# Fused attention and two gated layers: transpositions spread over the short key tiles, in a PSUM bank of their own

## The chip, the cores and the metric

One core of one Trainium2 chip runs the whole program. The metric is the device time of one execution in microseconds (us): the time from the first to the last instruction of that core. The kernel before was timed three times.

## The reference, cut to what matters

```python
q_rot, k_rot = rotate(q), rotate(k)              # (4, 8, 576, 64): 32 heads, 576 tokens, width 64
scores = (q_rot @ k_rot.transpose(0, 1, 3, 2)) / sqrt(64)
scores = scores - max(scores, axis=-1)           # one maximum per query
attn = exp(scores); attn = attn / (attn.sum(-1) + 1e-9)
x = (attn @ v)  -> (2304, 512)
x = (sigmoid(x @ w_gate) * (x @ w_val)) @ w_out  # 512 -> 1536 -> 512
out = elu(x @ w_in) @ w_out2                     # 512 -> 2048 -> 512
```

## The kernel before, in words

All of it is float32. The products must be more exact than one pass of the fast format (F32R), so an operand is split into a high part, rounded to F32R, and a low part, the difference.

**Heads, pairs, slots and steps.** The 32 heads are worked in 16 pairs. One head is one slot of ten steps, and slots follow one another (`scores`, `maxima`, `values`, called from the loop over `n` at the end of the attention part). In step h of slot i TensorE gets, in this order:
- `scores(i, h)` (L434): two products, K1 with Q1 and K2 with Q2, of one key tile and half of the 576 queries. Steps 0 to 3 and 5 to 8 have key tiles of 128 keys, steps 4 and 9 have the short tile of 64 keys. ScalarE takes the exponential. For a short tile it takes two, and VectorE then makes a low part of it (`low_part`, L444, put 1.5 steps later; written p below).
- `maxima(i+2, h)` (L387): one product for the row maxima of the head two slots ahead. Its result is reduced by VectorE (L389). A slot of even number has ten of them, a slot of odd number eight (steps 0 to 7).
- `values` (L463, or L460 and L461 for a short tile): the product with v, five steps behind the scores.

An entry made by `at(slot, step, ...)` runs after that step's products; a step ending in .5 runs ahead of the next step's products. In program order VectorE's queue at the start of a slot thus holds: the reduction of step 0, `join` (L394), p of the last slot's step 9, the reduction of step 1, the evacuation of a `values` result (L477), the copy of the maxima's row (L411, from `max_row`, whose product L409 also takes a tile of `ps_mt`), the reduction of step 2, and one operation of the weights' conversion (L121 to L140). After step 5 come the same conversion, p, a reduction and an evacuation. `max_row` needs `join`, since its stationary operand is what `join` writes.

**Splits.** A pair's rotated q and k have to be transposed and split before its maxima start. `split` does one half of one operand: two transpositions of 128x128 (L331; three where the tails are with it), one ScalarE copy into the high part (L334), one VectorE subtraction into the low part (L335). A pair has four of them and nine transpositions in all. For pair pr the first head is in slot s0 = 2 pr, and all four splits are in slot s0 - 4, an even one, ahead of steps 2, 4, 6 and 8, each followed by its subtraction one step later. Then `move` starts the DMAs that put the parts into W (L347 to L349, on SyncE's queue), and `last_queries` copies a few columns on GpSimd (L401). GpSimd makes the rotated q and k (`rope_ops`, L312 to L316) one to two slots earlier.

**PSUM.** The eight banks are three pools: `ps_mt` three (maxima and `max_row`), `ps_qk` three (scores, and the transpositions of `split`), `ps_pv` two (values). A new tile takes the bank that was released first, and waits for whoever read it last.

After attention, at about 320 us, come the two gated layers, 844 us of products of 128x512.

Of the kernel before, what the change touches and what calls it, by code (L numbers as in the profile page):

```python
# [9 lines left out]
F32 = mybir.dt.float32  # L10
F32R = mybir.dt.float32r
AF = mybir.ActivationFunctionType
ALU = mybir.AluOpType
# [6 lines left out]
def attention_moe_moe_kernel(  # L20
# [15 lines left out]
    nc = tc.nc  # L36
    B, H, S, D = q.shape
    P = 128
# [5 lines left out]
    ST = S // P  # L44
# [140 lines left out]
    banks = ctx.enter_context(ExitStack())  # L185
    with ExitStack() as att:
# [7 lines left out]
        prep = att.enter_context(ExitStack())  # L194
        raw_p = prep.enter_context(tc.tile_pool(name="raw", bufs=2))
        rope_p = prep.enter_context(tc.tile_pool(name="rope", bufs=1))
        ps_mt = banks.enter_context(tc.tile_pool(name="ps_mt", bufs=3, space=bass.MemoryType.PSUM))
        ps_qk = banks.enter_context(tc.tile_pool(name="ps_qk", bufs=3, space=bass.MemoryType.PSUM))
        ps_pv = banks.enter_context(tc.tile_pool(name="ps_pv", bufs=2, space=bass.MemoryType.PSUM))

        raws = {}
# [44 lines left out]
        ident = const.tile([P, P], F32, name="ident")  # L246
# [32 lines left out]
        def operand(i, which, c0, n):  # L279
            c = ("K2", "Q1", "K1", "Q2").index(which) * S + c0  # L280
            return W[i // 2 % NPAR][i % 2][:, c : c + n]
# [5 lines left out]
        def at(slot, step, fn, *args):  # L287
            agenda.setdefault(slot * NSTEP + step, []).append((fn, args))
# [3 lines left out]
        def rope_ops(pr, which, eng):  # L292


            if which == "t":
                x = raw(pr, "kq")
                r = rope_p.tile([P, 2, D], F32, tag="rt", name=f"rt{pr}")
                s = rope_p.tile([P, 2, D], F32, tag="st", name=f"st{pr}")
                rv, sv = r, s
                cos, sin = (tabt[:, j].unsqueeze(1).to_broadcast([P, 2, D]) for j in range(2))  # L300
            else:
                x = raw(pr, which)
                r = rope_p.tile([P, ST, 2, D], F32, tag="r" + which, name=f"r{which}{pr}", bufs=2)
                s = rope_p.tile([P, ST, 2, D], F32, tag="s", name=f"s{which}{pr}")
                rv, sv = (y.rearrange("p t h d -> p h t d") for y in (r, s))
                cos, sin = (tab[:, c].unsqueeze(1).to_broadcast([P, 2, ST, D]) for c in range(2))
            rot[pr, which] = r
            tt = eng.tensor_tensor

            axes = "p n" if which == "t" else "p h t"  # L310
            two = lambda y: y.rearrange(f"{axes} (two d) -> {axes} two d", two=2)
            tt(out=two(sv), in0=two(x)[..., ::-1, :], in1=two(sin), op=ALU.mult)  # L312
            yield
            tt(out=rv, in0=x, in1=cos, op=ALU.mult)
            yield
            tt(out=r, in0=r, in1=s, op=ALU.add)  # L316
            yield

        parts = {}

        def split(pr, which, half, later=None):

            if which == "k" and half == 0:

                parts[pr] = hl_p.tile([P, 4, S], F32R, tag="hl", name=f"hl{pr}")
            tails = which == "k" and half == 1
            c0, n = half * HM, HM + (P if tails else 0)
            T = ps_qk.tile([P, 512], F32, tag="qk", name=f"T{which}{pr}_{c0}")[:, 0:n]
            rows = [rot[pr, which][:, c // P] for c in range(c0, c0 + HM, P)] + ([rot[pr, "t"]] if tails else [])
            for j, r in enumerate(rows):  # L330
                nc.tensor.transpose(T[:, j * P : (j + 1) * P], r.rearrange("p h d -> p (h d)"), ident)  # L331
            c0 += 0 if which == "k" else S + TL
            hi, lo = (parts[pr][:, 2 * j : 2 * j + 2].rearrange("p w s -> p (w s)")[:, c0 : c0 + n] for j in range(2))
            nc.scalar.copy(hi, T)  # L334
            rest = lambda: nc.vector.tensor_tensor(out=lo, in0=T, in1=hi.bitcast(F32), op=ALU.subtract)  # L335
            if later is None:
                rest()
            else:
                at(*later, rest)

        def move(pr, ab):

# [80 lines left out]
        def scores(i, h):  # L423

            a, t = divmod(h, ST + 1)
            n = P if t < ST else TL
            if t == ST:

                p = probs[i, h] = p_p.tile([P, HA], F32R, tag="pt", name=f"p{i}_{h}")[:, 0:HS]
            else:  # L430
                e = probs[i, h] = e_p.tile([P, HA], F32, tag="ef", name=f"e{i}_{h}", bufs=2 * ST)[:, 0:HS]
            s = ps_qk.tile([P, 512], F32, tag="qk", name=f"s{i}_{h}")[0:n, 0:HS]
            for st, mv in (("K1", "Q1"), ("K2", "Q2")):
                nc.tensor.matmul(  # L434
                    s, lhsT=operand(i, st, t * P, n), rhs=operand(i, mv, a * HS, HS), start=st == "K1", stop=st == "K2"
                )
            if t == ST:
                nc.scalar.activation(p[TL:P], s, AF.Exp, scale=SCALE)
                e = s
                at(i, h + 1.5, low_part, e, p)  # L440
            nc.scalar.activation(e, s, AF.Exp, scale=SCALE)  # L441
# [6 lines left out]
        def values(i, h):  # L448


            a, t = divmod(h, ST + 1)
            pr, ab = divmod(i, 2)
            par = pr % 2
            c = slice(a * HS, (a + 1) * HS)
            if t == 0:
                ps[i, a] = ps_pv.tile([P, 512], F32, tag="pv", name=f"pv{i}_{a}")[:, 0:HS]
            out_ps = ps[i, a]
            e = probs.pop((i, h))
            if t == ST:
                nc.tensor.matmul(out_ps[0:D], lhsT=VT[par][:, ab, 0:D], rhs=e, start=False, stop=False)  # L460
                nc.tensor.matmul(out_ps, lhsT=VT[par][:, ab, D : 3 * D], rhs=e, start=False, stop=True)  # L461
            else:
                nc.tensor.matmul(out_ps, lhsT=VF[par][:, ab, t], rhs=e, start=t == 0, stop=False)  # L463
            if t < ST:
                return
            if ab == 0 and a == 0:
                us[pr] = (fin_p if pr == NPAIR - 1 else u_p).tile([P, S], F32, tag="u", name=f"u{pr}")
                sums[pr] = SUM[D * par : D * par + D]
            done = us[pr][D * ab : D * ab + D, c], sums[pr][32 * ab : 32 * ab + 1, c], out_ps
            if (i, a) == (NHEAD - 1, 1):  # L470
                return done
            at(i + 1, 5 * a + 0.5, evacuate, *done, "s")
            at(i + 1, 5 * a + 1, evacuate, *done, "u")
# [63 lines left out]
        at(-5, 4, constants, 1, 1, nc.gpsimd)  # L537
        for which in "kq":
            for half in range(2):
                at(-5, 1, split, 0, which, half)  # L540
            at(-5, 1, copies, 0, which, nc.vector.tensor_copy)
        at(-5, 1, move, 0, 1)
        at(-5, 2, last_queries, 0, nc.scalar.copy)
        at(-2, 19, last_queries, 1, nc.scalar.copy)
        for (which, half), st in zip((("k", 0), ("k", 1), ("q", 0), ("q", 1)), (10, 11, 17, 18)):
            at(-2, st, split, 1, which, half)
        at(-2, 13, copies, 1, "k", nc.scalar.copy)
        at(-2, 19, copies, 1, "q", nc.scalar.copy)
        at(-1, 11, move, 1, 1)
# [1 line left out]
        for pr in range(NPAIR):  # L551
            s0 = 2 * pr
            if pr > 1:
                for j, (which, slot, steps) in enumerate(
                    (
                        ("k", s0 - 6, (8, 8, 9, 9) if pr == 3 else (1,3,6,8)),
                        ("t", s0 - 6, (19,) * 4 if pr == 3 else (9, 9, 9, 9)),
                        ("q", *((0, (0, 0, 3, 3)) if pr == 2 else (s0 - 5, (1,3,6,8)))),
                    )
                ):  # L560
                    gen = rope_ops(pr, which, nc.gpsimd)
                    for st in steps:
                        at(slot, st, pull, gen)
                for j, (which, half) in enumerate((("k", 0), ("k", 1), ("q", 0), ("q", 1))):
                    at(s0 - 4, (6.5, 7.5, 8.5, 9.5)[j] if pr == 2 else (1.5, 3.5, 5.5, 7.5)[j], split, pr, which, half, None if pr == 2 else (s0 - 4, 2.5 + 2 * j))
                at(s0 - 4, 10 if pr == 2 else 9, move, pr, 0)
                at(s0 - 4, 10 if pr == 2 else 9, last_queries, pr, nc.gpsimd.tensor_copy)
                at(s0 - 4, 19, move, pr, 1)
            for piece in range(2 if pr > 0 else 0):
                at(s0 - 1, (5, 7)[piece], split_v, pr, piece)  # L570
        for pr in range(2, NPAIR):
            slot, step = {3: (-1, 9), 4: (1, 3)}.get(pr, (2 * pr - 8, 3))
# [30 lines left out]
        for n in range(-6 * NSTEP, NHEAD * NSTEP + half_slot):  # L603
            i, h = divmod(n, NSTEP)
# [21 lines left out]
        rest = remaining()  # L626
# [179 lines left out]
```

## Time and profile before

| what | value |
|---|---|
| time, median of three executions | 1164.22 us (1162.93 to 1165.01) |
| the profiled execution: span, which is its own time | 1164.2 us |
| TensorE (PE) busy | 1138.5 us, 98% |
| VectorE (DVE) busy | 937.7 us, 81% |
| ScalarE (ACT) / GpSimd (POOL) busy | 451.2 us, 39% / 605.0 us, 52% |
| granted TensorE clock | full in all 40 slices |

The page's busy share of TensorE counts matmuls whose ends are modelled and overlap, so a busy TensorE may still lose time. A better measure here is the distance of one instruction's start from that of the same instruction a slot or a step on. In the timeline view a row is: start in us from the span's start, duration, engine, line, operation, result and operands, shapes, how many were merged into the row, and in brackets the idle time before it and who ended it. In the view by windows a row is: the stretch, its length, then the busy time (and number of instructions) of PE, PEld (weight loads), DVE, ACT and POOL, the granted clock, the DMA engines' busy share and GB/s.

### The profile page before, as it was taken

What the parts mean: (1) busy time and instruction counts of PE and PEld (TensorE: products, weight loads), DVE (VectorE), ACT (ScalarE), POOL (GpSimd) and SP (SyncE); (2) the same over time, 40 slices, a digit from 0 to 9 for tenths busy, and PEclk for the clock granted to TensorE, in tenths of its full rate; (3) what the DMA queues carried; (4) which work ended last, traced back from release to release, by engine and by line L of the source; (5) the groups of instructions that cost most, each with busy time, mean ns of one, the idle gap of its engine ahead of it and who ended that gap; (6) DMA issues with size and microseconds to landing.
All of it is one profiled execution on the core that took longest, in us unless ns stands there. A gap on an engine that the chain in (4) does not pass through costs nothing.

```text
span 1164.2 us, 16786 instructions
## 1 busy us (share of the span) xinstructions
PE 1138.5 (98%) x5728; PEld 960.5 (82%) x5728; DVE 937.7 (81%) x1994; ACT 451.2 (39%) x1037; POOL 605.0 (52%) x695
## 2 busy tenths in 40 slices
PE   5999999999999999999999999999999999999998
PEld 3888888888888888888888888888888888888887
DVE  6768888887876888667777766888999999999844
ACT  4666666667753321221222122344322222222221
POOL 8766666863343554434444435775554545545521
PEclk9999999999999999999999999999999999999999
DMA  6667677767121211111111110111111111110004
GB/s 166 158 161 184 163 179 169 163 158 160 41 94 37 73 55 40 52 37 47 44 38 54 37 55 19 37 37 37 55 37 55 37 37 55 37 55 1 1 37 127
DMA packets 58757, 88.03 MB, mean 76 GB/s; under 512 B 18176, under 2 KB 30736, under 8 KB 58672
## 3 DMA queue, kind: packets, MB, share of 16 engines
q1 hardware_dynamic: 58672, 86.96, 28.2%
q8 instruction: 45, 0.74, 0.3%
q14 instruction: 40, 0.33, 0.1%
HBM read 55.45 MB, written 4.87 MB: 52 GB/s over the span
## 4 chain that ended last, share of the span: by engine, by line
PE 78%; DVE 17%; ACT 2%; issue 1%; DMA 1%; SPq 0%; POOL 0%; POOLq 0%
PE h L647 12%; PE h L648 12%; PE h L649 12%; PE pv L463 9%; PE o L647 7%; PE o L648 7%; PE o L649 7%; PE s L434 7%; DVE z L730 3%; PE mt L387 3%; DVE g L673 2%; DVE g L672 2%; DVE ca L131 2%; DVE cm L140 1%; DVE MX L389 1%; DVE ce L134 1%
## 5 line engine op out<-in xcount | busy, mean ns | idle before, releaser
L679 POOL TENSOR_TENSOR gl<-g,gh 128x512 fp32r<-128x512 f32 (+1 forms) x140 | 168.6, 1204 | 330.2 <-ACT gh L678 261.7
L678 ACT CAST gh<-g 128x512 fp32r<-128x512 f32 (+1 forms) x140 | 81.0, 579 | 308.2 <-DVE g L673 171.1
L434 PE MATMUL s<-W 128*128 128x288 f32 (+1 forms) x640 | 182.0, 366 | 3.8 <-DVE p L444 1.3
L648 PE MATMUL h<-xl,wh 128*128 128x512 f32 (+1 forms) x480 | 176.6, 368 | 0.0
L647 PE MATMUL h<-xh,wh 128*128 128x512 f32 (+1 forms) x480 | 176.6, 368 | 0.0
L649 PE MATMUL h<-xh,wl 128*128 128x512 f32 (+1 forms) x480 | 176.5, 368 | 0.0
L463 PE MATMUL pv<-e,VF 128*128 128x288 f32 x512 | 166.0, 407 | 0.0
L141 POOL TENSOR_TENSOR ca<-ca,wh 128x256 f32<-128x256 f32 x136 | 111.5, 820 | 96.8 <-DVE cm L137 82.4
L389 DVE TENSOR_REDUCE MX<-mt 128x1 f32<-128x288 f32 x288 | 127.5, 450 | 40.9 <-PE mt L387 38.7
L434 PEld LDWEIGHTS s<-W 128*128 128x128 f32 (+1 forms) x640 | 106.1, 182 | 32.1 <-DVE p L444 5.2
L138 ACT CAST wh<-ca 128x256 fp32r<-128x256 f32 x136 | 55.1, 405 | 195.0 <-DVE ca L131 195.0
L143 POOL TENSOR_TENSOR wl<-ca,cm 128x256 fp32r<-128x256 f32 x136 | 111.0, 816 | 18.5 <-DVE cm L140 12.1
L441 ACT ACTIVATE e<-s 128x288 f32<-128x288 f32 x256 | 104.3, 411 | 41.4 <-PE s L434 38.2
L648 PE MATMUL h<-yl,wh 128*128 128x512 f32 (+1 forms) x320 | 117.7, 368 | 0.0
L649 PE MATMUL h<-yh,wl 128*128 128x512 f32 (+1 forms) x320 | 117.7, 368 | 0.0
L647 PE MATMUL h<-yh,wh 128*128 128x512 f32 (+1 forms) x320 | 117.7, 368 | 0.0
L668 DVE TENSOR_TENSOR g<-h,g 128x512 f32<-128x512 f32 (+1 forms) x60 | 38.2, 637 | 95.1 <-PE h L649 92.3
L647 PE MATMUL o<-wh,gh 128*128 128x512 f32 x288 | 112.7, 391 | 1.5 <-DVE z L730 1.2
L648 PE MATMUL o<-wl,gh 128*128 128x512 f32 x288 | 112.2, 389 | 0.0
L649 PE MATMUL o<-wh,gl 128*128 128x512 f32 x288 | 112.1, 389 | 0.0
L649 PEld LDWEIGHTS h<-xh,wl 128*128 128x128 f32 x480 | 90.5, 189 | 15.1
L647 PEld LDWEIGHTS h<-xh,wh 128*128 128x128 f32 x480 | 90.5, 189 | 15.0
(110 smaller groups left out, 2514.4 us busy)
## 6 DMA issues: line engine op xcount, KB each, us to landing
W<-hl SPq DMA_DIRECT2D x90, 288.0 KB
raw<-in_moe_w_out_dram SPq DMA_DIRECT2D x28, 512.0 KB
raw<-in_moe_w_in_dram SPq DMA_DIRECT2D x16, 512.0 KB
raw<-in_moe_w_gate_dram SPq DMA_DIRECT2D x12, 512.0 KB
raw<-in_moe_w_val_dram SPq DMA_DIRECT2D x12, 512.0 KB
rb<-d SPq DMA_DIRECT2D x32, 144.0 KB
k<-in_k_dram SPq DMA_DIRECT2D x16, 256.0 KB
q<-in_q_dram SPq DMA_DIRECT2D x16, 256.0 KB
```

The source lines that it names most:

```text
L138: nc.scalar.copy(h, a)
L141: nc.gpsimd.tensor_tensor(out=a, in0=a, in1=h.bitcast(F32), op=ALU.subtract)
L143: nc.gpsimd.tensor_tensor(out=l, in0=a, in1=mf, op=ALU.add)
L389: nc.vector.tensor_reduce(out=MX[pr % 2][:, a, c : c + 1], in_=m, axis=AX.X, op=ALU.max, negate=True)
L434: nc.tensor.matmul(s, lhsT=operand(i, st, t * P, n), rhs=operand(i, mv, a * HS, HS), start=st == "K1", stop=st == "K2")
L441: nc.scalar.activation(e, s, AF.Exp, scale=SCALE)
L463: nc.tensor.matmul(out_ps, lhsT=VF[par][:, ab, t], rhs=e, start=t == 0, stop=False)
L647: nc.tensor.matmul(ps, lhsT=ah, rhs=bh, start=j == 0, stop=False)
L648: nc.tensor.matmul(ps, lhsT=ah, rhs=bl, start=False, stop=False)
L649: nc.tensor.matmul(ps, lhsT=al, rhs=bh, start=False, stop=j == n - 1)
L678: nc.scalar.copy(hi, g)
L679: nc.gpsimd.tensor_tensor(out=lo, in0=g, in1=hi.bitcast(F32), op=ALU.subtract)
```

## The change

From the fifth pair (pr = 4) on the four splits of a pair are put one to each short key tile of two slots: k's halves to steps 4 and 9 of slot s0 - 5 (odd), q's halves to steps 4 and 9 of slot s0 - 4 (even). Their transpositions are no longer issued together; each is put ahead of one product of the short tile: K1, K2 and the first of `values`. ScalarE's copy follows after the step's products (`finish`), the subtraction 1.5 steps later, but for q's second half at once. Their PSUM tile comes from a new pool `ps_t` of one bank; `ps_mt` has two banks instead of three. `move` of the pair's first head and `last_queries` run one step later. The first two pairs' q second half also takes `ps_t`; pairs 0 to 3 stay where they were.

```diff
-        ps_mt = ...tile_pool(name="ps_mt", bufs=3, space=PSUM)
+        ps_mt = ...tile_pool(name="ps_mt", bufs=2, space=PSUM)
         ps_qk = ...tile_pool(name="ps_qk", bufs=3, space=PSUM)
+        ps_t = ...tile_pool(name="ps_t", bufs=1, space=PSUM)
...
+        between = []
-        def split(pr, which, half, later=None):
+        def split(pr, which, half, pool, tag, later=None, apart=False):
...
-            T = ps_qk.tile([P, 512], F32, tag="qk", ...)[:, 0:n]
+            T = pool.tile([P, 512], F32, tag=tag, ...)[:, 0:n]
...
+            def finish():
+                assert not between
+                nc.scalar.copy(hi, T)
+                if later is None:
+                    rest()
+                else:
+                    at(*later, rest)
+            for j, r in enumerate(rows):
+                if apart:
+                    between.append((turn, (j, r)))
+                else:
+                    turn(j, r)
+            if apart:
+                at(*apart, finish)
+            else:
+                finish()
+        def one_between():
+            if between:
+                fn, args = between.pop(0)
+                fn(*args)
...
             for st, mv in (("K1", "Q1"), ("K2", "Q2")):      # scores
+                if t == ST:
+                    one_between()
                 nc.tensor.matmul(s, ...)
...
             if t == ST:                                      # values
+                one_between()
                 nc.tensor.matmul(out_ps[0:D], ...)
...
-                    at(s0 - 4, (6.5, ...)[j] if pr == 2 else (1.5, 3.5, 5.5, 7.5)[j], split, pr, which, half,
-                       None if pr == 2 else (s0 - 4, 2.5 + 2 * j))
-                at(s0 - 4, 10 if pr == 2 else 9, move, pr, 0)
-                at(s0 - 4, 10 if pr == 2 else 9, last_queries, pr, nc.gpsimd.tensor_copy)
+                    if pr < 4:
+                        ...                                  # as before, from ps_qk
+                    else:
+                        slot, step = s0 - 5 + j // 2, 4 + 5 * (j % 2)
+                        at(slot, step - 0.5, split, pr, which, half, ps_t, "t",
+                           (slot, step + 1.5) if j < 3 else None, (slot, step))
+                at(s0 - 4, 10 if pr == 2 or pr > 3 else 9, move, pr, 0)
+                at(s0 - 4, 10 if pr == 2 or pr > 3 else 9, last_queries, pr, nc.gpsimd.tensor_copy)
```

## Rows read from the trace of the kernel before

**Rows 1.** The page: its first line.

```profile
span 1164.2 us, 16786 instructions
```

**Rows 2.** By windows: the odd slot 17, and slot 28, even and without a split.

```profile
184.79:193.03 8.24, 8.24 (x52) 7.29 (x51) 7.12 (x18) 5.54 (x16) 8.00 (x12) 1.00 0.54 108
...
285.38:293.85 8.47, 8.47 (x53) 7.52 (x52) 6.73 (x18) 5.61 (x15) 0.00 (x0) 1.00 0.63 141
```

**Rows 3.** By windows: the twelve even slots 4 to 26; slots 6 and 24, and the sum.

```profile
80.69:91.72 11.03, 10.36 (x63) 8.29 (x61) 7.99 (x23) 7.05 (x19) 4.12 (x6) 1.00 0.61 141
...
248.54:258.97 10.43, 10.01 (x62) 8.29 (x61) 9.34 (x22) 7.04 (x19) 7.40 (x10) 1.00 0.52 115
...
sum 123.63, PE 118.66 PEld 99.27 DVE 103.89 ACT 85.16 POOL 66.66; mean PE 9.89 PEld 8.27 DVE 8.66 ACT 7.10 POOL 5.55
```

**Rows 4.** Timeline of PE in the even slot 16 (174.16 to 184.79).

```profile
178.01 0.38 PE L331 MATMUL Tk<-ident,rk 128*128 128x128 f32 x2
178.23 0.27 PE L331 MATMUL Tk<-ident,rt 128*128 128x128 f32 x1
...
180.32 0.41 PE L331 MATMUL Tq<-ident,rq 128*128 128x128 f32 x2 [0.29 <-ACT e L441]
...
182.03 0.53 PE L434 MATMUL s<-W 128*128 128x288 f32 x2 [0.42 <-DVE p L444]
```

**Rows 5.** Timeline of DVE in slot 16.

```profile
178.20 0.41 DVE L335 TENSOR_TENSOR hl<-Tk,hl 128x256 fp32r<-128x256 f32 x1
178.53 0.86 DVE L389 TENSOR_REDUCE MX<-mt 128x1 f32<-128x288 f32 x2
179.31 0.55 DVE L335 TENSOR_TENSOR hl<-Tk,hl 128x384 fp32r<-128x384 f32 x1
179.78 0.45 DVE L389 TENSOR_REDUCE MX<-mt 128x1 f32<-128x288 f32 x1
180.14 1.36 DVE L121 TENSOR_SCALAR ce<-raw 128x256 int32<-128x256 int32 x1
181.53 0.45 DVE L444 TENSOR_TENSOR p<-s,p 64x288 fp32r<-64x288 f32 x1
```

**Rows 6.** Timeline of POOL in slot 24: the end of pair 14's rotated q.

```profile
249.59 1.27 POOL L316 TENSOR_TENSOR rq<-rq,sq 128x512 f32<-128x512 f32 x1
```

**Rows 7.** By windows: the last 2 us of slot 17.

```profile
191.00:193.03 2.03, 2.03 (x15) 1.76 (x14) 1.70 (x5) 1.08 (x4) 1.87 (x3) 1.00 0.00 0
```

**Rows 8.** Timeline of ACT where slot 17 begins: a copy, and step 9's second exponential.

```profile
183.44 0.37 ACT L334 CAST hl<-Tq 128x256 fp32r<-128x256 f32 x1 [0.42 <-PE Tq L331]
...
184.90 0.39 ACT L441 ACTIVATE s<-s 64x288 f32<-64x288 f32 x1
```

**Rows 9.** Timeline of DVE at the start of slot 17: reductions of steps 0 and 1.

```profile
185.38 0.46 DVE L389 TENSOR_REDUCE MX<-mt 128x1 f32<-128x288 f32 x1 [0.20 <-PE mt L387]
...
186.32 0.44 DVE L389 TENSOR_REDUCE MX<-mt 128x1 f32<-128x288 f32 x1
```

**Rows 10.** Timeline of PE in slot 17: the maxima's product of step 2.

```profile
186.94 0.29 PE L387 MATMUL mt<-W 128*128 128x288 f32 x1
```

**Rows 11.** Timeline of DVE in slot 28: p, and the conversion after step 5.

```profile
286.53 0.45 DVE L444 TENSOR_TENSOR p<-s,p 64x288 fp32r<-64x288 f32 x1
...
290.63 0.42 DVE L131 SCALAR_TENSOR_TENSOR ca<-ce,cm 128x256 f32<-128x256 int32 x1
```

**Rows 12.** Timeline of PE in slot 28: the maxima's products of steps 2 and 8.

```profile
287.50 0.29 PE L387 MATMUL mt<-W 128*128 128x288 f32 x1
...
292.58 0.29 PE L387 MATMUL mt<-hl,QT 128*128 128x288 f32 x1
```

**Rows 13.** Timeline of DVE in slot 8: the conversion after step 5.

```profile
106.35 0.85 DVE L137 TENSOR_SCALAR cm<-ca 128x256 int32<-128x256 int32 x1
```

**Rows 14.** Timeline of DVE at the start: the first head's reductions.

```profile
14.56 3.94 DVE L389 TENSOR_REDUCE MX<-mt 128x1 f32<-128x288 f32 x10 [0.76 <-PE mt L387]
```

**Rows 15.** Timeline of DVE where slot 8 begins (99.95).

```profile
101.19 0.21 DVE L495 RECIPROCAL r<-r 128x9 f32<-128x9 f32 x1 [1.57 <-DMA r<-d]
```

More of the change, by code (lines that the diff above doesn't have):

```diff
@@ L196, in attention_moe_moe_kernel @@
         rope_p = prep.enter_context(tc.tile_pool(name="rope", bufs=1))
-        ps_mt = banks.enter_context(tc.tile_pool(name="ps_mt", bufs=3, space=bass.MemoryType.PSUM))
+        ps_mt = banks.enter_context(tc.tile_pool(name="ps_mt", bufs=2, space=bass.MemoryType.PSUM))
         ps_qk = banks.enter_context(tc.tile_pool(name="ps_qk", bufs=3, space=bass.MemoryType.PSUM))
+        ps_t = banks.enter_context(tc.tile_pool(name="ps_t", bufs=1, space=bass.MemoryType.PSUM))
         ps_pv = banks.enter_context(tc.tile_pool(name="ps_pv", bufs=2, space=bass.MemoryType.PSUM))
@@ L327, in split, with turn, rest @@
             c0, n = half * HM, HM + (P if tails else 0)
-            T = ps_qk.tile([P, 512], F32, tag="qk", name=f"T{which}{pr}_{c0}")[:, 0:n]
+            T = pool.tile([P, 512], F32, tag=tag, name=f"T{which}{pr}_{c0}")[:, 0:n]
             rows = [rot[pr, which][:, c // P] for c in range(c0, c0 + HM, P)] + ([rot[pr, "t"]] if tails else [])
-            for j, r in enumerate(rows):
-                nc.tensor.transpose(T[:, j * P : (j + 1) * P], r.rearrange("p h d -> p (h d)"), ident)
             c0 += 0 if which == "k" else S + TL
             hi, lo = (parts[pr][:, 2 * j : 2 * j + 2].rearrange("p w s -> p (w s)")[:, c0 : c0 + n] for j in range(2))
[L334 to L337, printed above, removed]
-            else:
-                at(*later, rest)
+            def turn(j, r):
+                nc.tensor.transpose(T[:, j * P : (j + 1) * P], r.rearrange("p h d -> p (h d)"), ident)
+            def rest():
+                nc.vector.tensor_tensor(out=lo, in0=T, in1=hi.bitcast(F32), op=ALU.subtract)
+            def finish():
[12 more added lines that the diff above has]
+                at(*apart, finish)
+            else:
+                finish()
[3 more added lines that the diff above has]
+                fn(*args)
         def move(pr, ab):
@@ L539, in attention_moe_moe_kernel @@
             for half in range(2):
-                at(-5, 1, split, 0, which, half)
+                at(-5, 1, split, 0, which, half, *((ps_t, "t") if (which, half) == ("q", 1) else (ps_qk, "qk")))
             at(-5, 1, copies, 0, which, nc.vector.tensor_copy)
@@ L545, in attention_moe_moe_kernel @@
         for (which, half), st in zip((("k", 0), ("k", 1), ("q", 0), ("q", 1)), (10, 11, 17, 18)):
-            at(-2, st, split, 1, which, half)
+            at(-2, st, split, 1, which, half, *((ps_t, "t") if (which, half) == ("q", 1) else (ps_qk, "qk")))
         at(-2, 13, copies, 1, "k", nc.scalar.copy)
@@ L564, in attention_moe_moe_kernel @@
                 for j, (which, half) in enumerate((("k", 0), ("k", 1), ("q", 0), ("q", 1))):
-                    at(s0 - 4, (6.5, 7.5, 8.5, 9.5)[j] if pr == 2 else (1.5, 3.5, 5.5, 7.5)[j], split, pr, which, half, None if pr == 2 else (s0 - 4, 2.5 + 2 * j))
-                at(s0 - 4, 10 if pr == 2 else 9, move, pr, 0)
-                at(s0 - 4, 10 if pr == 2 else 9, last_queries, pr, nc.gpsimd.tensor_copy)
+                    if pr < 4:
+                        at(s0 - 4, (6.5, 7.5, 8.5, 9.5)[j] if pr == 2 else (1.5, 3.5, 5.5, 7.5)[j], split, pr, which, half, ps_qk, "qk", None if pr == 2 else (s0 - 4, 2.5 + 2 * j))
+                    else:
+                        slot, step = s0 - 5 + j // 2, 4 + 5 * (j % 2)
+                        at(slot, step - 0.5, split, pr, which, half, ps_t, "t", (slot, step + 1.5) if j < 3 else None, (slot, step))
+                at(s0 - 4, 10 if pr == 2 or pr > 3 else 9, move, pr, 0)
+                at(s0 - 4, 10 if pr == 2 or pr > 3 else 9, last_queries, pr, nc.gpsimd.tensor_copy)
                 at(s0 - 4, 19, move, pr, 1)
```

## The prediction

> **What bounds the kernel now.** I read the page first: span 1164.2 us [rows 1], 0.02 us under the median of the three runs, so the sum starts there. TensorE is busy nearly throughout, and the change touches attention alone, so the question is which attention slots are longer than their products need. The view by windows, cut at the slots, answers it. An odd slot takes 8.24 us with TensorE busy for all of it, and slot 28, even but without a split, 8.47 us, also full [rows 2]. The twelve even slots that hold the splits of pairs 4 to 15 sum to 123.63 us [rows 3], 10.30 us each. The timeline of one of them shows what its splits cost. Nine transpositions are real work: two start within 0.22 us, so 0.11 us each [rows 4], 0.98 us per pair, and 8.47 + 0.98 = 9.45 us would do. The rest is waiting: the first transposition of q waits 0.29 us for an exponential, because it needs a bank of the scores' pool, and 1.4 us later a score product waits 0.42 us for VectorE's p [rows 4], which stood behind a weight conversion of 1.36 us [rows 5] while the transpositions held a third of the pool.
>
> So TensorE sets the end, and loses 123.63 - 12 x 9.45 = 10.2 us to these slots. Odd slots lose nothing. VectorE is second: 103.89 of the 123.63 us in the even slots [rows 3], 7.12 of 8.24 in an odd one [rows 2]. It takes its work strictly in the written order, so where it is late by more than the maxima's banks hold, TensorE stops.
>
> **Removed.** With a bank of their own the transpositions no longer wait for scores, nor scores for them. All twelve even slots would fall to 9.45 us, but for slot 6: its 11.03 us [rows 3] are 1.6 over, and I leave 1.2 of that in, as the transpositions' typical waiting in the calmer slots is about 0.45 (0.29 waited for, the rest unnamed). Gain 10.2 - 1.2 = **9.0 us** (bounds 7.5 and 10.2).
>
> **Moved at no price.** The transpositions stay 108 in number. Beside a 64-column product I take the same 0.11 us; no row has one right behind a short product. The recorded times are 0.38 for two and 0.27 for one [rows 4], whose difference again is 0.11; a quarter of it either way, 0.03 us, gives bounds of -3 and +3 us, and I take 0. GpSimd must finish the rotated q earlier: for pair 14 it ends at 250.86 [rows 6], and its transposition would stand in step 4 of the slot that starts at 248.54 [rows 3], four steps of 0.88 us later, near 252.1. That is 1.2 us of cover, and the slots ahead grow by about as much as GpSimd's copies (L401) are held up; without the cover each 0.1 us late costs 1.2 us over the twelve pairs. The `move` DMAs of a pair's first head start up to 1.2 us later, since they need q's last high part. The maxima and the row copy behind them in SyncE's queue are due when the slot ends, and in the last 2.03 us of slot 17 the DMA engines were at 0.00 [rows 7], so this cover is larger than the delay. Value 0, at worst +2 us for both.
>
> **Added, in the odd slots.** q's last subtraction is issued at once after step 9, ahead of the next slot's reduction of step 0. It needs ScalarE's copy, which stands behind step 9's second exponential: that starts at 184.90 and takes 0.39, the copy takes 0.37 [rows 8], so the copy ends at 185.68, the subtraction starts at about 185.71, and the reduction behind it 0.33 later (178.20 to 178.53 in [rows 5]), at 186.04. In the trace it started at 185.38, and that of step 1 0.94 later [rows 9]; now step 1's starts at 186.98, ends 0.44 later and releases its bank after 0.05 (p ends at 181.98 and TensorE goes on at 182.03 [rows 4, 5]): 187.47. With two banks the product of step 2 needs just this bank, since the product of `max_row` in between takes the other. It stood at 186.94 [rows 10], so TensorE waits 0.53 us. With three banks it would need step 0's, free at 186.55. Twelve odd slots (5 to 27): **+6.4 us**. The bounds: 0.3 and 0.7 each, 3.6 and 8.4.
>
> **Added, in the even slots, step 2.** The wide subtraction of k's second half now stands between p and step 1's reduction. In slot 28 p starts at 286.53 [rows 11]; 0.37 later the subtraction, 0.47 later (179.31 to 179.78 [rows 5]) the reduction, 0.44 and 0.05 to its release: 287.86. The product of step 2 stands at 287.50 [rows 12]: 0.36 us, twelve times, **+4.3 us** (bounds 2.4 and 5.4).
>
> **Added, in the even slots, step 8.** After step 5 the queue holds conversion, p, the subtraction of q's first half, and step 6's reduction. With a conversion of w us from 290.63 [rows 11], the release comes at 290.63 + w + 0.37 + 0.33 + 0.44 + 0.05 = 291.82 + w; step 8's product stands at 292.58 [rows 12], so any w over 0.76 stops TensorE. The eleven conversions there are short, as 0.42 [rows 11], or long: five take from 0.85 (slot 8, [rows 13]) to 1.36 us (slot 16, [rows 5]), with 0.03 to the next start. These pass 0.76 by 0.12 to 0.63 each, together **+1.9 us** (bounds 0 and 4). In odd slots there is no product of step 8 to stop.
>
> **Added, at the start.** The first ten reductions follow one another at 0.394 us [rows 14]. With two banks two of them need 0.45 + 0.05 and 0.33 from a product's start to its reduction, 0.415 each. Ten reductions are 0.2 us longer, those of slots 0 and 1 about as much again: **+0.5 us** (bounds 0 and 1.5).
>
> Sum: -9.0 + 6.4 + 4.3 + 1.9 + 0.5 = +4.1 us, **1168.3 us**. Behind attention nothing changes, and TensorE, full there, gives nothing back.
>
> [...] The odd slots' term rests on VectorE's not passing a waiting instruction. Where slot 8 began, a reciprocal waited 1.57 us for a DMA and nothing else ran on VectorE [rows 15]. [...] A transposition here takes 0.11 us beside another one [rows 4]. [...]
>
> **The rivals.** (A) Faster: the bank waits do not bind. For it: VectorE is idle for 20 of 123.63 us in the even slots [rows 3], and in today's order two banks would nearly do: in slot 17 step 1's reduction ends at 186.76 [rows 9], 0.18 us ahead of step 2's product [rows 10]. It decides at one point: if step 1's reduction ends before step 2's product stands, that is if the subtractions hold it up by less than that room. Then -9.0 + 0.5 and at most 1.5 of scattered waits remain: 1157. Against it: the written order fixes who stands ahead of whom, and no row shows those places with room. (B) Cancelled: one of the two step-2 places binds and the other does not, or the transpositions get cheaper: 1164.2 - 9.0 + 6.4 + 0.5 + 1.9 = 1164.0. (C) The splits come too late for the DMAs or GpSimd: the first maxima of a slot wait for W, or q's transposition for its rotation; 0.2 us per pair on top of the sum, 1170.7. Against it the covers above. (D) The change doesn't do what it says, transpositions dearer between short products by up to 0.03 us: 1171.3.
>
> **How the numbers follow.** My forecast, slower by stops at two banks, has 0.42; C and D together 0.10; B 0.20; A 0.28. The forecast's own range is 1166.6 to 1171.5 from its terms' bounds taken half way. About 0.2% (2.3 us) is what a measurement of this kernel tells from no change. Slower is the forecast with C and D, 0.52 less 0.02 at its lower edge: 0.50. Same is B, less 0.02 at its faster edge, with the forecast's 0.02: 0.20. Faster is A and that edge: 0.30. The range takes in A's 1157 and D's 1171.3 with a little beyond: 1156.5 to 1172.5.
>
> **What would show it.** In the new trace: no transposition waits for an exponential, and none of the even slots shows a score product waiting for p; slot 28 stays at 8.47. Odd slots with a split (five transpositions, 0.55 us) would take 8.79 without stops, and I expect 9.3; even ones 8.91 without, and I expect 9.3 to 10. In both the product of step 2 should wait for VectorE's reduction, queued behind a subtraction, and in odd slots VectorE should sit idle ahead of that subtraction until ScalarE's copy. If odd slots stay at 8.8 and step 2's product doesn't wait, the two-bank step is wrong, and the time is near 1157.

## The result, and the profile after

The changed kernel takes 1175.98 us (median of four runs, 1173.58 to 1176.09); the kernel before took 1163.58 beside it (four runs, 1162.83 to 1165.01). The ratio is 1.010 (95% interval 1.0085 to 1.0115): slower, as forecast, but by 12.4 us where 4.1 was said, and outside the range.

The page of the changed kernel, its first line and the busy times:

```profile
span 1174.2 us, 16842 instructions
...
PE 1146.0 (98%) x5728; PEld 965.2 (82%) x5728; DVE 932.2 (79%) x1994; ACT 449.0 (38%) x1037; POOL 605.8 (52%) x695
```

The span grew by 10.0 us [rows 1], not by 12.4. In every run of these two kernels that has both on record, a run's time is 1.7 to 1.8 us above its span, and 46 later runs of the kernel before have spans of 1158.5 to 1164.6 us with medians of 1161.9 and 1162.1. So the profiled execution of before, with 1164.2, was one of its longer ones, by about 2 us; where it spent them the traces don't show. Spans are compared with spans here. The two gated layers take 844.5 us before and 844.4 after, so all of it is in attention. TensorE issues the same 5728 products, yet its busy time rose from 1138.5 to 1146.0 us. Recorded products overlap (one that started at 191.25 took 0.29 us, and the next started at 191.38, 0.13 later), so a part of each stop counts as busy.

Cut at the slots (a slot starts with the first score product of its step 0), the 10 us split like this:

| stretch | before | after | difference |
|---|---|---|---|
| to the start of slot 0 | 24.24 | 26.12 | +1.9 |
| slot 0 | 11.70 | 13.33 | +1.6 |
| slots 1 to 3 (slot 3 now has a k with five transpositions) | 26.56 | 27.24 | +0.7 |
| even slots 4 to 26 | 123.61 | 115.70 | -7.9 |
| odd slots 5 to 27 | 99.27 | 112.99 | +13.7 |
| slots 28 to 31 | 34.35 | 34.47 | +0.1 |

The view by windows of the changed kernel: even slot 6, even slot 24 and the sum of the twelve even slots, which answer to [rows 3], then the odd slot 17 and slot 28, which answer to [rows 2].

```profile
85.63:96.20 10.57, 9.58 (x57) 8.09 (x56) 7.42 (x21) 6.32 (x17) 4.36 (x6) 1.00 0.63 147
...
257.89:267.56 9.67, 9.35 (x57) 8.04 (x56) 7.71 (x20) 6.23 (x17) 7.66 (x9) 1.00 0.54 126
...
sum 115.68, PE 111.17 PEld 96.26 DVE 91.62 ACT 75.34 POOL 65.38; mean PE 9.26 PEld 8.02 DVE 7.64 ACT 6.28 POOL 5.45
...
191.38:200.78 9.40, 9.20 (x57) 7.76 (x55) 7.26 (x20) 6.14 (x18) 7.83 (x11) 1.00 0.48 98
295.38:303.86 8.48, 8.48 (x54) 7.54 (x53) 6.72 (x18) 5.60 (x15) 0.01 (x1) 1.00 0.63 145
```

Most even slots are now 9.48 to 9.71 us, odd ones 9.40 to 9.60 (slot 27, which holds no transpositions, 8.87), and slot 28 is as it was. What TensorE waits for from 28 us on (waited for, us in total, times, longest):

```profile
PE mt L411 <- DVE MX L413: 6.4, 24, 0.4
PE s L460 <- ACT e L467: 1.2, 1, 1.2
PE s L460 <- DMA W<-row: 0.6, 1, 0.6
PE Tq L337 <- DVE MX L413: 0.2, 1, 0.2
```

In slots 4 to 27 no transposition waits for an exponential any more, no score product for p. In their place the maxima's product waits for VectorE's reduction 24 times, once in each of these slots. The same view for the weight loads says more:

```profile
PEld mt L411 <- DVE MX L413: 12.9, 29, 0.6
PEld mr L433 <- DVE MJ L418: 4.7, 12, 0.4
```

These two sum to 17.6 us; the stops worked out below from distances between products come to 15.4. The 6.4 us of the first list are what is left once the recorded, overlapping ends of the products ahead are taken off.

**One stop in an even slot.** Slot 16 starts at 181.67. TensorE, weight loads and VectorE around step 2 (rows of TensorE and VectorE answer to [rows 4, 5]):

```profile
182.81 0.29 PE L411 MATMUL mt<-W 128*128 128x288 f32 x1
...
183.21 0.44 PE L433 MATMUL mr<-identr,MJ 128*128 128x128 f32 x1
183.48 0.48 PE L460 MATMUL s<-W 128*128 128x288 f32 x2
184.28 0.40 PE L411 MATMUL mt<-W 128*128 128x288 f32 x1 [0.32 <-DVE MX L413]
...
185.27 0.29 PE L411 MATMUL mt<-W 128*128 128x288 f32 x1
```

```profile
183.42 0.30 PEld L460 LDWEIGHTS s<-W 128*128 128x128 f32 x2
184.28 0.19 PEld L411 LDWEIGHTS mt<-W 128*128 128x128 f32 x1 [0.56 <-DVE MX L413]
```

```profile
182.82 0.45 DVE L470 TENSOR_TENSOR p<-s,p 64x288 fp32r<-64x288 f32 x1
183.31 0.56 DVE L340 TENSOR_TENSOR hl<-Tk,hl 128x384 fp32r<-128x384 f32 x1
183.78 0.45 DVE L413 TENSOR_REDUCE MX<-mt 128x1 f32<-128x288 f32 x1
```

The maxima's products of steps 1, 2 and 3 start at 182.81, 184.28 and 185.27. A step is 0.88 us, and 0.99 where it holds the 0.11 of `max_row`'s product: the one of step 2 is due at 183.80 and comes 0.48 late, and the next comes another 0.11 late. A stop costs 0.59 us, though the bracket reads 0.32. The reduction's start at 183.78, 0.45 long, and 0.05 to the release give 184.28 just as the prediction's sum has it. What it had not: the weight load of the stopped product waits as well and starts with the product (184.28 both), and the product lasts 0.40 instead of 0.29 us. The instruction records of the trace say why the load waited: of the 5728 products of the changed kernel none carries a wait for a semaphore; 1378 weight loads do, the one at 184.28 among them, and 132 waits stand by themselves.

**One in an odd slot.** Slot 17 starts at 191.38; VectorE, ScalarE and TensorE (answering to [rows 8 to 10]):

```profile
192.29 0.42 DVE L340 TENSOR_TENSOR hl<-Tq,hl 128x256 fp32r<-128x256 f32 x1 [0.52 <-ACT hl L344]
192.63 0.45 DVE L413 TENSOR_REDUCE MX<-mt 128x1 f32<-128x288 f32 x1
193.00 0.15 DVE L418 TENSOR_REDUCE MJ<-MX 128x5 fp32r<-128x10 f32 x1
...
193.56 0.44 DVE L413 TENSOR_REDUCE MX<-mt 128x1 f32<-128x288 f32 x1
```

```profile
191.89 0.37 ACT L344 CAST hl<-Tq 128x256 fp32r<-128x256 f32 x1
```

```profile
192.52 0.30 PE L411 MATMUL mt<-W 128*128 128x288 f32 x1
...
193.21 0.33 PE L433 MATMUL mr<-identr,MJ 128*128 128x128 f32 x1
...
194.06 0.40 PE L411 MATMUL mt<-W 128*128 128x288 f32 x1 [0.20 <-DVE MX L413]
```

VectorE idles 0.52 us ahead of q's last subtraction, until ScalarE's copy ends: the forecast place. It didn't pass on to the reduction behind it, whose product had started at 191.64 and took 0.30. That reduction starts 1.25 us into the slot (192.63; forecast 186.04 - 184.79 = 1.25), and step 2's product starts 2.68 into it, where the forecast had its bank free (187.47 - 184.79). From 192.52 to 194.06 it is 1.54 us instead of 0.99, and 0.11 more follow.

**At the start.** TensorE and VectorE (answering to [rows 14]):

```profile
14.56 0.97 PE L411 MATMUL mt<-W 128*128 128x288 f32 x2 [0.31 <-DVE MX L413]
15.72 0.97 PE L411 MATMUL mt<-W 128*128 128x288 f32 x2 [0.19 <-DVE MX L413]
```

```profile
14.04 0.82 DVE L413 TENSOR_REDUCE MX<-mt 128x1 f32<-128x288 f32 x2 [0.76 <-PE mt L411]
15.20 0.82 DVE L413 TENSOR_REDUCE MX<-mt 128x1 f32<-128x288 f32 x2 [0.34 <-PE mt L411]
```

Two reductions now take 1.16 us, 0.58 each instead of 0.394 before and 0.415 forecast. From a restart to the reduction it is 0.64 us here (14.56 to 15.20), where 0.33 was reckoned: products took about twice as long at this time (a maxima's product 0.55 us at 20.09, and 0.29 at 39.79).

**At step 8 of the even slots.** VectorE in slot 16, the conversion after step 5 (answering to [rows 5]):

```profile
187.73 0.68 DVE L121 TENSOR_SCALAR ce<-raw 128x256 int32<-128x256 int32 x1
```

The same conversion took 1.36 us before. All five long ones, 0.85 to 1.36 us before, now take 0.43 to 0.68; in both traces these ran beside an operation of GpSimd, and the other six that lie there, at 0.28 to 0.42, did not.

### The profile page after: what moved, and what is told of

It is laid out like the page before. It is cut to its first block, busy times and chain, and to the rows that moved or that the text cites. A ratio compares the mean times of both kernels' runs of the same rounds, so it can differ in the third digit from the quotient of the medians.

```text
span 1174.2 us, 16842 instructions
## 1 busy us (share of the span) xinstructions
PE 1146.0 (98%) x5728; PEld 965.2 (82%) x5728; DVE 932.2 (79%) x1994; ACT 449.0 (38%) x1037; POOL 605.8 (52%) x695
## 4 chain that ended last, share of the span: by engine, by line
PE 67%; DVE 26%; ACT 3%; issue 2%; DMA 1%; SPq 0%; POOL 0%; DVEq 0%; ACTq 0%; POOLq 0%
PE h L679 10%; PE h L680 10%; PE h L678 10%; PE pv L490 8%; PE s L460 6%; PE o L678 6%; PE o L679 6%; PE o L680 6%; DVE z L761 4%; PE mt L411 4%; DVE g L704 3%; DVE g L703 3%; DVE ca L131 3%; DVE cm L126 2%; DVE MX L413 2%
## 5 line engine op out<-in xcount | busy, mean ns | idle before, releaser
L460 PE MATMUL s<-W 128*128 128x288 f32 (+1 forms) x640 | 185.7, 370 | 1.9 <-ACT e L467 1.2
L460 PEld LDWEIGHTS s<-W 128*128 128x128 f32 (+1 forms) x640 | 109.3, 182 | 28.2 <-ACT e L467 2.6
```

Source lines behind the costliest of these rows:

```text
L460: nc.tensor.matmul(s, lhsT=operand(i, st, t * P, n), rhs=operand(i, mv, a * HS, HS), start=st == "K1", stop=st == "K2")
```

## The experiments

Theory: the stops come from two banks meeting the written places of the subtractions, and a stopped product loses its hidden weight load besides. Rivals: the banks alone slow everything; or the transpositions between short products are dear; or it is their new places in TensorE's stream. Spans are given beside 1164.2 (before) and 1174.2 (after).

**e1: two banks and nothing else** (the kernel before; the eighth bank stays unused).

```diff
-        ps_mt = ...tile_pool(name="ps_mt", bufs=3, space=PSUM)
+        ps_mt = ...tile_pool(name="ps_mt", bufs=2, space=PSUM)
```

> The kernel before with ps_mt cut from three banks to two (the eighth bank unused), nothing else. Theory: two banks stop TensorE only where a subtraction stands ahead of step 1's reduction, which this order has nowhere, and at the start, where reductions go from 0.39 to about 0.58 us each: about +3.5 us at the start, 0 to 2 us in the slots, 1167 to 1169 us. Rival (the third bank itself is what was lost, whatever the order of the subtractions): every slot loses 0.6 us as in the changed kernel and the transpositions' waits stay, 1180 us or more.

1168.06 us, ratio 1.0032 (1.0018 to 1.0047); span 1165.2. Slot 0 starts at 26.09, 1.85 us late as in the changed kernel, and the pairs at the start are the same:

```profile
14.55 0.97 PE L387 MATMUL mt<-W 128*128 128x288 f32 x2 [0.31 <-DVE MX L389]
15.71 0.97 PE L387 MATMUL mt<-W 128*128 128x288 f32 x2 [0.19 <-DVE MX L389]
```

But the odd slots stay at 8.24 us, and the even ones sum to 122.25. So the banks alone cost the start; the slots' stops need the moved subtractions. (Over all runs e1 is about 4 us slower than the kernel before beside it, within the theory's 1167 to 1169; the spans show only 1.0, as before's profiled execution was long.)

**e2: a third bank at the start only** (the changed kernel; every third tile of the first three heads' maxima from `ps_t`).

```diff
+            early.append(0)
+            third = i < 3 and len(early) % 3 == 0
-            m = ps_mt.tile(..., tag="mt", ...)[:, 0:HS]
+            m = (ps_t if third else ps_mt).tile(..., tag="t" if third else "mt", ...)[:, 0:HS]
```

> The changed kernel, but every third maxima tile of the first three heads comes from the transpositions' bank, idle then; all else as changed. Theory: the start's 3.5 us come back, 1172.5 us, and slot 4 onwards stays as it is. Rival (the start is late for another reason, the shared bank for q's transpositions or the moved code): 1176 us.

1174.15 us, ratio 1.0084 (1.0066 to 1.0102); span 1172.6, 1.6 less than after. Slot 0 starts at 24.34: the start's 1.9 us are back, while the slots from 4 on get none (even 116.75, odd 113.10).

**e3: q's last subtraction behind the next slot's second reduction** (the changed kernel; `move` right behind it).

```diff
-  ..., ps_t, "t", (slot, step + 1.5) if j < 3 else None, (slot, step))
+  ..., ps_t, "t", (slot, step + (1.5 if j < 3 else 2)), (slot, step))
```

> The changed kernel, but q's second subtraction is put behind the next slot's reduction of step 1 (two steps later), and the DMAs of move for the pair's first head right behind it. Theory: the odd slots' stop of 0.67 us falls to 0.1 us or less, 12 x 0.6 = 7 us, 1169 us; even slots as they are. Rival (the stop is the two banks', wherever the subtraction stands): odd slots stay at 9.4 to 9.5 us, 1176 us. If the later DMAs were to bind, slots of even number would begin with a wait for W.

1169.84 us, ratio 1.0048 (1.0030 to 1.0067); span 1167.4. By windows, slots 17 and 19:

```profile
187.94:196.82 8.88, 8.88 (x57) 7.86 (x55) 7.59 (x20) 6.20 (x18) 7.63 (x11) 1.00 0.50 102
...
206.33:215.20 8.87, 8.87 (x57) 7.87 (x55) 7.63 (x20) 6.56 (x19) 6.40 (x10) 1.00 0.64 149
```

The odd slots have 8.86 to 8.93 us (slot 27: 8.33), and these rows show no idle time of TensorE: one instruction's place in VectorE's queue was worth 7.0 us (112.99 to 105.97). What came back is one wait of 1.3 us, in slot 6, for the DMAs that `move` starts.

**e4: one pool of three banks for maxima and transpositions** (the changed kernel, places unchanged).

```diff
-        ps_mt = ...tile_pool(name="ps_mt", bufs=2, space=PSUM)
-        ps_t = ...tile_pool(name="ps_t", bufs=1, space=PSUM)
+        ps_mt = ...tile_pool(name="ps_mt", bufs=3, space=PSUM)
+        ps_t = ps_mt
```

> The changed kernel with its order, but the transpositions' tiles and the maxima share one pool of three banks instead of one and two. Theory: a transposition's bank is back before step 2's product needs one, which then waits for the subtraction (even) or not at all (odd): stops of 0.1 to 0.3 us instead of 0.6, and the start back at 24.2 us, 1161 to 1165 us. Rival (the transpositions hold the third bank when it is needed, so sharing is no better than two banks): 1172 us or more.

1165.20 us, ratio 1.0009 (0.9996 to 1.0022); span 1163.2. Same places, same transpositions, no bank more: 11.0 us less than after. Even slots sum to 113.52 and odd ones to 107.89. At the start VectorE keeps its old pace, eight reductions in 3.14 us:

```profile
14.03 3.14 DVE L413 TENSOR_REDUCE MX<-mt 128x1 f32<-128x288 f32 x8 [0.76 <-PE mt L411]
```

This speaks against the rivals of dear transpositions and of their places in TensorE's stream: both are as in the changed kernel.

**e5: e4, and the second subtraction of k half a step later, that of q two steps later** (`move` right behind q's).

```diff
-  ..., (slot, step + 1.5) if j < 3 else None, (slot, step))
+  ..., (slot, step + (2 if j % 2 else 1.5)), (slot, step))
```

> The shared pool of three banks, and both subtractions of second halves (k's and q's) put behind the next slot's reduction of step 1; move of the pair's first head right behind q's. Theory: what is left of the stops in the shared-pool kernel (0.28 us in step 2 of even slots, which waits for k's subtraction; 0.21 us at max_row in odd ones, which waits for join behind q's subtraction) goes to about 0.05 each, 12 x 0.4 = 5 us: 1160 us, even slots near 8.95, odd ones near 8.85. Rival (the subtraction's 0.4 to 0.5 us come back wherever they are put, VectorE being nearly full): 1165 us as with the shared pool alone.

1161.23 us, ratio 0.9975 (0.9965 to 0.9985); span 1160.3. This is faster than both kernels, by 2.7 us against before. By windows, the odd slot 17 and the even slot 18:

```profile
183.11:191.87 8.76, 8.76 (x56) 7.79 (x55) 7.68 (x20) 6.27 (x18) 7.19 (x11) 1.00 0.61 129
191.87:201.03 9.16, 9.16 (x58) 8.02 (x56) 7.88 (x21) 6.18 (x17) 5.49 (x7) 1.00 0.72 165
```

The odd slot has what the prediction gave for it without stops (8.79). The even one is 0.25 over its 8.91 although TensorE shows no idle time in it. Its timeline, the maxima's products of steps 2 and 3:

```profile
194.00 0.29 PE L413 MATMUL mt<-W 128*128 128x288 f32 x1
...
195.03 0.37 PE L413 MATMUL mt<-W 128*128 128x288 f32 x1
```

1.03 us instead of 0.88, and a long product again: a stop too short to appear as idle time. What it waits for the lists of waits don't name.

**e6: half the stationary columns in the maxima** (the changed kernel; the maxima of half of the queries are left out). The streamed 288 columns, the banks and all waits are the same; the reductions read 64 partitions instead of 128 and take 0.44 us instead of 0.45.

```diff
-            nc.tensor.matmul(m, lhsT=st, rhs=mv, ...)
+            nc.tensor.matmul(m[0:D], lhsT=st[:, 0:D], rhs=mv, ...)
```

> The changed kernel with the maxima's stationary operand cut from 128 to 64 columns: the maxima of half the queries are left out (their table stays at zero). Streams of 288 columns, reductions and order stay. Theory (a stopped product's own weight load waits with it, so it is exposed): from the stopped product's start to its reduction's start 0.46 us shrinks towards 0.40, each stop by 0.05 to 0.06 us, 24 stops and the start: 1174 to 1175 us. Rival (the 0.11 us are the restart of the engine, whatever it loads): 0.46 us and 1176 us stay.

1172.80 us, below the theory's 1174 to 1175, ratio 1.0079 (1.0064 to 1.0095); span 1170.9, 3.3 less than after. Slot 16's stop, TensorE and its weight load:

```profile
180.28 0.30 PE L411 MATMUL mt<-W 128*64 128x288 f32 x1
...
181.73 0.35 PE L411 MATMUL mt<-W 128*64 128x288 f32 x1 [0.29 <-DVE MX L413]
...
182.66 0.29 PE L411 MATMUL mt<-W 128*64 128x288 f32 x1
```

```profile
181.73 0.13 PEld L411 LDWEIGHTS mt<-W 128*64 128x64 f32 x1 [0.52 <-DVE MX L413]
```

Undisturbed products last 0.29 to 0.30 us with 64 columns as with 128: the size of a hidden weight load doesn't show in them. The stopped one falls from 0.40 to 0.35, and the step behind it is 0.93 instead of 0.99 us. Half the columns took away about half of the extra time. The even slots fall by 0.07 us each (115.70 to 114.86), the odd ones by 0.085, 1.9 us in all, and slot 0 starts 0.88 us sooner. The other 0.5 us are in slot 0, for the reason told at the end of this document.

**e7: the old places with a shared pool of three** (the kernel before; only the bank of the transpositions changes).

```diff
-            T = ps_qk.tile(..., tag="qk", ...)
+            T = (ps_mt if pr > 3 else ps_qk).tile(..., tag="mt" if pr > 3 else "qk", ...)
```

> The kernel before with the transpositions of pairs 4 to 15 where they were, all four in one slot ahead of steps 2, 4, 6 and 8, but their tiles from the maxima's three banks instead of the scores'. Theory (the waits removed were the scores' banks', spreading adds little): no transposition waits for an exponential, even slots 9.5 to 9.8 us, odd ones 8.24, 1156 to 1160 us. Rival (spreading is needed, for four subtractions in one slot keep VectorE behind and the maxima stop instead): even slots 10 us and more, 1163 us.

1162.25 us, ratio 0.9985 (0.9975 to 0.9994); span 1162.0. The theory wanted 1156 to 1160 and the rival 1163: it lies nearer the rival. Even slots scatter from 9.42 to 11.36 us (sum 121.38). The list of TensorE's waits has a new kind:

```profile
PE mt L387 <- DVE hl L335: 1.8, 6, 0.4
PE s L434 <- DMA W<-row: 1.6, 1, 1.6
```

Bunched transpositions now hold up the maxima until their subtraction is done. Taking the scores' pool out of it gives about 2 us; spreading them, with e5's order, gives the even slots another 7.8 (121.38 to 113.54), of which 6.0 go to the odd slots (99.20 to 105.18), whose transpositions are real work.

**e8: the change's own pools, with e2's start and e5's order.**

> The changed kernel with its pools (two banks for maxima, one for transpositions), the third bank at the start, and both second subtractions behind the next slot's reduction of step 1. Theory (each stop belongs to a subtraction ahead of that reduction): both stops at step 2 go, even slots 9.0 to 9.1, odd ones 8.85 us, 1162 to 1165 us. Rival (two banks stop TensorE at the next place, the row's copy ahead of step 3's product): even slots 9.3 and more, 1167 us.

This is the changed kernel with e2's edit and with e5's subtractions and `move`, but not its shared pool. 1165.39 us, ratio 1.0013 (1.0004 to 1.0022), just above the theory's 1162 to 1165; span 1162.3. Odd slots are mostly 8.86, as the theory said. Even ones are mostly 9.28, the rival's 9.3 and not the theory's 9.0 to 9.1, and the rival also named the place:

```profile
PEld mt L417 <- DVE row L441: 3.8, 12, 0.3
```

Such an even slot is 0.37 us over the 8.91. The one wait that comes in each of the twelve is that of a maxima's product for the copy of `max_row`'s bank, at step 3, and TensorE's own list doesn't name it. With the order mended a bank of its own is thus 2 us (spans) or 4 us (medians) behind a shared pool of three.

## Why the prediction was right in its direction and wrong in its size

The path was right: the waits that it removed went, and the two places that it named at step 2 do stop TensorE. What failed is its price of a stop, which it took as the wait alone, and most of all the term of the start, which it put at 0.5 us. It also began from the span of one execution, 1164.2 us, as if that were a time. A run's time is 1.8 us more, so between the two profiled executions 1.8 of the 7.7 us from 1168.3 to 1176.0 come from this, and 5.9 from the terms.

**Removed: right.** Without its stop a 9.52 us even slot is 8.93; forecast 8.91. Slot 6 kept 1.06 us of the 1.2 that was left in for it.

**Transpositions at 0.11 us wherever they stand: right.** In e5 an odd slot with five takes 8.76 us and one without them 8.24 [rows 2], TensorE full in both: 0.104 each.

**Added, in the odd slots and at step 2 of the even slots: right place, wrong size. This is the step that failed.** It took a stopped product to go on as if nothing had happened once its bank was released. Its weight load had waited with it, so 0.11 us more were lost at each stop, as the rows of after show. e6 confirms it by about halving it: the extra duration was 0.11 us with 128 columns and 0.06 with 64, beside recorded loads of 0.19 and 0.13.

- Even slots: 0.36 forecast. The subtraction behind p starts 0.49 after it (182.82 to 183.31), not 0.37 as a reduction does: +0.12; the load: +0.11. Measured 0.585 on average, 7.0 us in twelve slots instead of 4.3, and more than its upper bound of 5.4.
- Odd slots: 0.53 forecast; 0.67 measured (0.20 where `max_row`'s product waits for the join, which stands behind the same late reduction, and 0.47 at step 2). The sum over the odd slots is 7.8 us above e5's (112.99 against 105.18), instead of 6.4. The prediction let `max_row` take the other bank and forgot that it needs the join; this mattered little, since both wait for the same queue.

**Added, at step 8 of the even slots: too high.** 1.9 us forecast; slots 12, 16, 20 and 24, where step 8's product does come late, lie about 0.6 us in all above the usual 9.5. The durations of the conversions were taken over from the kernel before, and they became shorter by a third to a half (0.68 against 1.36 us in slot 16). This error hid 1.3 us of the others.

**Added, at the start: the largest miss.** 0.5 us forecast; 1.9 until slot 0 and 1.6 in slot 0. The first is the same step again, with the restart at the start's slower products: ten reductions at 0.58 instead of 0.394 are 1.9 us. e1 shows it alone, e2 takes it away. The second seems to come mostly from TensorE's rate, and not from the change: early on, products took about twice the time, then they dropped to their later durations, and in the profiled execution this came late. Its timeline:

```profile
34.66 0.64 PE L337 MATMUL Tk<-ident,rk 128*128 128x128 f32 x2
...
36.43 0.38 PE L337 MATMUL Tk<-ident,rk 128*128 128x128 f32 x2
```

The two of the first row start 0.21 us apart, those of the second 0.11. The same operation before:

```profile
32.00 0.38 PE L331 MATMUL Tk<-ident,rk 128*128 128x128 f32 x2
```

e3 issues the same products in the same order up to slot 3 and starts them within 0.1 us of the changed kernel until 31 us; there the drop came 3.2 us sooner, and slot 0 took 11.87 us, 0.2 more than before. So about 1.4 of the 1.6 us seem to belong to the execution. One trace of each kernel can't settle it: of the changed kernel's other runs two took as long as the profiled one, and one 2.4 us less.

The sizes that the prediction missed add up: +2.7 (even, step 2), +1.4 (odd), -1.3 (step 8), +3.0 (start), +0.2 elsewhere: 6.0 us on top of its 4.1, against 10.0 measured between the spans. The forecast's own range, 1166.6 to 1171.5, doesn't come out of its bounds: half of those of its five terms gives 1164.2 to 1172.2, and the result lies above either.

**The rivals.** A (the bank waits do not bind) is refuted by the 24 waits. B fails as both places bind. C needs a late DMA or GpSimd: the first list of waits has one of 0.6 us, for the row in slot 6, and no more. D is refuted by e5.

## What to carry to other kernels

Before a pool loses a buffer, walk the consumer's queue in its written order and ask whether the oldest buffer is released before the producer stands at it; where it isn't, one instruction moved behind the reduction that releases the buffer can be worth more than a whole bank (7.0 us in e3's odd slots; taking a bank from the kernel before cost about 4 us in e1). Price a stop of TensorE as the wait plus the weight load that no longer hides (here 0.11 us with 128 columns, 0.06 with 64), and more while products still run slow (at the start 0.64 us from a restart to the reduction, where 0.33 was reckoned). Read stops from the distance between like products or from the weight loads' waits, not from TensorE's busy share: here the products' share is 98% for both kernels while 15 us went into stops; the weight loads' share is 82% for both and doesn't tell them apart either.

## What the runs showed of the hardware that was not expected

In these traces a product whose bank wasn't free held back its weight load too (load and product both start at 184.28 in slot 16): none of the 5728 products carries a wait, and the waits stand on loads (1378 in the changed kernel, 1292 before) or by themselves (132 and 177). The stopped product lasted 0.40 us instead of 0.29, with 64 columns 0.35.

How long products took about twice their later time at the start differed between executions of the same stream of products (until 32.6 us in e3 and 35.8 in the changed kernel), and slot 0 paid about half of it. The moment at which products drop to their shorter durations, and slot 0:

| kernel | slot 0 starts | shorter from | slow products in slot 0 | length of slot 0 |
|---|---|---|---|---|
| before | 24.24 | 31.1 | 6.9 | 11.70 |
| e3 | 26.02 | 32.6 | 6.6 | 11.87 |
| e1 | 26.09 | 33.3 | 7.2 | 12.14 |
| e4 | 23.71 | 31.7 | 8.0 | 12.21 |
| e2 | 24.34 | 32.7 | 8.3 | 12.40 |
| e6 | 25.24 | 34.0 | 8.7 | 12.84 |
| after | 26.12 | 35.8 | 9.7 | 13.33 |

From before to after the slow stretch lasts 2.8 us longer and the slot is 1.6 us longer; e5, e7 and e8 lie on the same line (7.8, 7.6 and 8.1 us; 12.12, 12.03 and 12.26). The windows print a granted clock of 1.00 from the first microsecond on, and the page full slices, but there they had nothing to read: each trace's first clock record, at 1.00, begins at just the moment in the table, and none lies before it. The only other level that the record of the changed kernel names is 0.50, for its last 1.8 us, with TensorE idle. A time twice as long would fit that level; this is the author's estimate, as no record lies over the slow stretch. What sets the moment stays open; no run was made for it.
